# Blocks 2 and 3 of a delta-rule kernel inverted as a pair, their key Grams computed in the head

## The chip, the cores and the metric

The kernel runs on one core of a Trainium2 chip. The metric is the device time of one execution in microseconds (us): 607.63 as the median of three runs of the kernel before (606.84, 611.45, 607.63).

## The reference

The reference computes a delta-rule attention over 4 batches, 8 heads, 768 tokens and head size 48, and puts its output, as 3072 tokens of 384 features, through a feed-forward layer with 2048 hidden features:

```python
k_n = k / (norm(k) + 1e-06)
for t in range(S):
    y[:, :, t] = q[:, :, t] @ state
    v_old = state @ k_n[:, :, t]
    state = state + beta[t] * outer(k_n[:, :, t], v[:, :, t] - v_old)
x = y.transpose(0, 2, 1, 3).reshape(B * S, H * D)
h = x @ w_in
out = maximum(0.01 * h, h) @ w_out
```

Everything is float32.

## The kernel before

**Blocks.** The 768 tokens are cut into 12 blocks of 64. In a block the recurrence of each of the 32 sequences (4 batches by 8 heads) is solved by matrices: the Gram of its 64 keys gives a triangular matrix L, whose inverse T turns keys and values into updates of the state. T is inverted as two halves of 32 tokens each, and the part between them (the corner) is put together afterwards by products with the squares (step pz and pu, L501 and after).

**Per block.** `gram(n)` (L280) loads the keys and queries (kq, L288), multiplies keys with keys and queries in one matmul of 128 columns (pg, L308), copies the key part to gs (ScalarE, L312), stores it to DRAM as gd (L316) and loads it back as L in the layout of the inversion (L346); VectorE masks the query part into rq (L325) and copies the corners into gm (L333). `inv(b)` (L406) eliminates L over 31 steps on VectorE (`eliminate`, L391 and L396). A single block uses 16 columns of T at a time and all 128 partitions; the pair of blocks 0 and 1 uses 32 columns, in one inversion. `solve(n)` (L592) then makes the outputs ys of block n (pk, pw, py, px) and the new state (pc).

**The inverse's way out.** For the pair [0, 1], T is transposed on VectorE (tc, L442, and in place, L448) and copied from there by `place` (L484). For a single block, ScalarE reorders T (L456), SyncE stores it as td and tt (L462, L463), and DMAs load the squares sq (L468, L472) and the halves rt (L537) from these.

**The feed-forward layer.** `ffn(n)` (L739) takes 16 steps of 128 hidden features: ph (L759), Prelu into gh on ScalarE (L769), po (L750). Block 0 takes the weights as plain float32 (one product). From block 1 on inputs, hidden values and weights are each split into a high and a low part, and there are three products, with xl (L128) and gl (L774) as low parts, both made on VectorE.

**Weights.** Eight loads of 1536 KB (wr, `load_w`, L137) bring the weights in a 16-bit layout. Per load j: `pack(j)` (ScalarE, L152), `conv(j)` (four VectorE instructions, L162 to L165), `expand(j)` (ScalarE, L172), `final(j)` (VectorE, L179), after which block 0 can use them; then `cast(j)` (ScalarE, L186) and `lows(j)` (VectorE, L193) make the two parts for block 1 and after. The head issues loads 0 to 3, and 4 to 7 come during block 0.

**What sets the order.** The program is written as generators that are woven by hand: a loop over blocks and over 17 steps s each takes one step of `ffn`, then the work that a table (L860) sets for this step, then steps of `solve` (n + 1), of `inv` and of `gram` by the tables SV, IV, GG and G4. Each engine runs its instructions in the order in which they come out, and `behind(mark)` puts an instruction after a marked one of another engine. All loads and most stores stand in one queue, SyncE's; each of its DMAs waits, by the program's semaphores, for the landing of the one eight places ahead of it. In the head (before block 0): `first()` makes the Grams of blocks 0 and 1, `inv(0)` runs on VectorE beside the loads, `fetch(0, g)` (L570, L572) loads keys, values and queries of block 0, and dummy matmuls (`warm`) run on TensorE towards the end of the inversion.

Of the kernel before, what the change touches and what calls it, by code (L numbers as in the profile page):

```python
# [47 lines left out]
def delta_moe_kernel(ctx: ExitStack, tc, kq0, kqT, kv, qT, beta, cst, w_all, out, nblk):  # L48
# [44 lines left out]
    NB = [[0, 1]] + [[n] for n in range(2, nblk)]  # L93
# [186 lines left out]
    def gram(n):  # L280
        need(sv, "y", n - Q_BUFS // NGR)
        kqs = []
        for g in range(NGR):
            t = sb.tile([P, GS, NPAIR, 2, C], F32, tag="kq", name=f"kq{n}_{g}", bufs=KQ_BUFS)
            kqs.append(t)
            with behind("L" if n > BG + 1 else "kq"):
                for b in range(2):
                    nc.sync.dma_start(t[b * R0:b * R0 + D].rearrange("p s u x t -> p (s u x t)"), kqT[n, g, b])  # L288
        if n == GS:
            yield  # L290
# [4 lines left out]
        for g in range(NGR):  # L295
            kq = kqs[g]
# [3 lines left out]

            ps = [ps_a.tile([P, 512], F32, tag="a", name=f"pg{n}_{g}_{b}") for b in range(2)]
            pv = [x.rearrange("p (u x t) -> p x u t", u=NPAIR, x=2) for x in ps]
            for p in range(NPAIR):
                for c in range(2):
                    for b in range(2):
                        r = slice(b * R0, b * R0 + D)
                        with behind("ph") if n > 2 else nullcontext():
                            nc.tensor.matmul(ps[b][c * 64:(c + 1) * 64, p * 128:(p + 1) * 128],  # L308
                                             kq[r, c ^ b, p, 0], kq[r, c ^ b, p].rearrange("p x t -> p (x t)"),
                                             start=True, stop=True)  # L310
            for b in range(2):
                nc.scalar.copy(gs[:, b], pv[b][:, 0])  # L312
            for c in range(2):
                for e in range(2):
                    a = e * HS + g * GH + c * GU
                    queue.dma_start(  # L316
                        gd[a:a + GU].rearrange("l j i -> j l i"),
                        gs[c * 64 + e * HC:c * 64 + (e + 1) * HC].rearrange("p b u t -> p (b u) t")[:, :, e * HC:(e + 1) * HC])

            def masked(pv=pv, qa=of("q", n, g), to=DATA[g]):  # L320
                for b in range(2):
                    for c in range(2):
                        r = slice(c * 64, (c + 1) * 64)
                        with behind("gl") if n > 2 else nullcontext():
                            nc.vector.tensor_tensor(  # L325
                                qa[to, c, b * NPAIR:(b + 1) * NPAIR], pv[b][r, 1],
                                tri[r].rearrange("p (o t) -> p o t", o=1).broadcast_to([C, NPAIR, C]), ALU.mult)

            def corners(g=g, gs=gs):
                for c in range(2):  # L330
                    k = 2 * g + c
                    with behind("gl") if n > 2 else nullcontext():
                        nc.vector.tensor_copy(gm[n][k * HC:(k + 1) * HC].rearrange("p (b u) t -> p b u t", b=2), gs[c * 64:c * 64 + HC, :, :, HC:])  # L333

            if n == 2:
                masked()
                corners()
            elif not g:
                masked()
                held.append(corners)  # L340
            else:
                tails.extend([[masked], held + [corners]])
                held.clear()
            if g == NGR - 1:
# [4 lines left out]
                if n > GS:  # L349
                    mark["L"] = i.ins  # L350
# [30 lines left out]
    def eliminate(b, L, j, T, m):  # L381
# [13 lines left out]
        for tv, t in parts:  # L395
            mark["steps"] = nc.vector.tensor_tensor(t, t, tv, ALU.subtract).ins  # L396
# [9 lines left out]
    def inv(b):  # L406

        if b:
            need(gg, gram, NB[b][0])
# [4 lines left out]
        if two:  # L414
# [16 lines left out]
        if two:  # L431
            for n in NB[b]:
                lengths(n)
        yield
        for j in range(HC - 1):
            eliminate(b, L, j, T, j + 1 if two else j // 2 + 1)
            if two and j in WARM:
                warm(T[:, 0], WARM[j])
            if j == HC - 2:
                if two:  # L440
# [12 lines left out]
                else:  # L453
                    n = NB[b][0]
                    Tt = X[:, M * HC:].rearrange("p (i m) -> p i m", m=M)
                    nc.scalar.copy(Tt.rearrange("p i m -> p m i"), T)  # L456
                    td = dr.tile([2, HS, HC, HC], F32, tag="td", name=f"td{n}")
                    tt = dr.tile([HS, HC, HC], F32, tag="tt", name=f"tt{n}")
                    Tts[n] = td, tt
                    for x in range(2):  # L460
                        a = x * 64
                        nc.sync.dma_start(tt.rearrange("l i (x m) -> x l i m", m=M)[x], Tt[a:a + HS])  # L462
                        nc.sync.dma_start(td.rearrange("e l m i -> (e l) m i")[:, x::2], T[a:a + 64])  # L463
                    A, B = square(0), square(1)
                    queue = nc.gpsimd if b > BG else nc.sync
                    for k in range(4):
                        r = slice(k * HC, (k + 1) * HC)
                        mark["A"] = queue.dma_start(A[r, :, r], tt[k * GU:(k + 1) * GU].rearrange("u i m -> i u m")).ins  # L468
                    for v in range(4):
                        r = slice(v * HC, (v + 1) * HC)  # L470
                        with behind("A" if b > BG else None):
# [490 lines left out]
```

## Time and profile before

| | before |
|---|---|
| median of 3 runs | 607.63 us (606.84 to 611.45) |
| profiled execution | 607.1 us |
| its span, first to last instruction | 605.3 us |
| TensorE (PE) busy | 564.8 us, 93% |
| VectorE (DVE) busy | 448.7 us, 74% |
| ScalarE (ACT) busy | 311.3 us, 51% |
| GpSimd (POOL) busy | 77.8 us, 13% |
| mean granted TensorE clock | 0.991 |
| share of the chain that ended last | PE 73%, DVE 16%, DMA 4% |

The profile is of one execution. Times in it are us from the first instruction. A timeline row merges neighbouring instructions of one kind: its start, how long the group took, engine, line and operation, output<-input, the shape, and how many; behind it in brackets is how long the engine stood idle before it, and what ended that. The waits view sums such idle times. DMA-issuing instructions stand on their queue's engine (SPq is SyncE's), and the time to landing is given apart. The chain is followed back from the last instruction, step by step, to what released each.

### The profile page before, as it was taken

To read this page: it belongs to the slowest core of one execution; us is meant where nothing else is said; L and a number is where in the kernel's file an instruction comes from. 1 tells how busy PE (TensorE), PEld (TensorE's weight loads), DVE (VectorE), ACT (ScalarE), POOL (GpSimd) and SP (SyncE) were. 2 spreads that over 40 slices of the span, in tenths; PEclk is the share of its full clock that TensorE was granted. 3 is DMA by queue.
4 is the path that set the end of the run, shared out by engine and by line. 5 is a ranking of instruction groups with operands and counts; after the bars stand their busy time and mean duration, and the time that the engine had idled before them with its cause. 6 is when DMAs were issued, how large, how long until landed. Compare 5 with 4: busy or idle time off the path is not lost.

```text
span 605.3 us, 22381 instructions
## 1 busy us (share of the span) xinstructions
PE 564.8 (93%) x9146; PEld 518.2 (86%) x9146; DVE 448.7 (74%) x1981; ACT 311.3 (51%) x786; POOL 77.8 (13%) x135
## 2 busy tenths in 40 slices
PE   5287989889899999999999999999999999999996
PEld 4266767678799999999999999999999999999996
DVE  3999899978848969859859869769779679341221
ACT  3287976744546446436445445445445445454432
POOL 7000000100140040040130130130120210210100
PEclk9987999999999999999999999999999999999999
DMA  5994942244290273381481490490491450410100
GB/s 124 303 286 174 341 95 60 51 86 83 83 187 8 50 118 109 65 182 32 72 181 23 74 194 9 78 195 16 67 195 29 73 123 2 83 34 3 28 1 27
DMA packets 104423, 59.69 MB, mean 99 GB/s; under 512 B 92544, under 2 KB 93632, under 8 KB 103296
## 3 DMA queue, kind: packets, MB, share of 16 engines
q1 hardware_dynamic: 99168, 50.32, 37.5%
q0 software_dynamic: 4576, 7.22, 5.4%
q8 instruction: 72, 1.18, 0.9%
q10 hardware_dynamic: 576, 0.72, 0.6%
q14 instruction: 31, 0.25, 0.2%
HBM read 46.96 MB, written 11.27 MB: 96 GB/s over the span
## 4 chain that ended last, share of the span: by engine, by line
PE 73%; DVE 16%; DMA 4%; issue 3%; ACT 2%; SPq 1%; DVEq 0%; POOL 0%; ACTq 0%
PE po L750 30%; PE ph L759 29%; DVE tmp L391 3%; DVE T L396 3%; PE pw L656 3%; PE py L693 3%; PE pg L308 2%; DVE w L193 2%; DMA tt<-T 2%; PE pk L631 2%; DVE cg L179 2%; PE pc L631 1%; PE px L728 1%; DVE rq L325 1%; DMA sq<-tt 1%
## 5 line engine op out<-in xcount | busy, mean ns | idle before, releaser
L759 PE MATMUL ph<-xh,w 128*128 128x256 f32 x1056 | 203.9, 284 | 0.0
L750 PE MATMUL po<-w,gh 128*128 128x384 f32 x704 | 180.0, 345 | 0.0
L769 ACT ACTIVATE gh<-ph 128x256 fp32r<-128x256 f32 (+1 forms) x192 | 73.5, 385 | 202.6 <-PE ph L759 121.2
L759 PEld LDWEIGHTS ph<-xh,w 128*128 128x128 f32 x1056 | 168.1, 188 | 2.7 <-issue 2.0
L774 DVE TENSOR_TENSOR gl<-ph,gh 128x256 fp32r<-128x256 f32 x176 | 74.3, 423 | 108.4 <-ACT ph L773 103.3
L759 PE MATMUL ph<-xl,w 128*128 128x256 f32 x528 | 148.4, 283 | 1.8 <-DVE xl L128 1.8
L750 PEld LDWEIGHTS po<-w,gh 128*128 128x128 f32 x704 | 120.2, 188 | 3.7 <-issue 1.4
L750 PE MATMUL po<-w,gl 128*128 128x384 f32 x352 | 112.9, 339 | 2.4 <-DVE gl L774 2.4
L396 DVE TENSOR_TENSOR T<-T,tmp 128x60 f32<-128x60 f32 (+35 forms) x661 | 110.8, 207 | 0.7
L391 DVE TENSOR_TENSOR tmp<-T,L 128x60 f32<-128x60 f32 (+35 forms) x661 | 110.8, 208 | 0.6
L759 PEld LDWEIGHTS ph<-xl,w 128*128 128x128 f32 x528 | 99.5, 188 | 2.6 <-DVE xl L128 2.2
L750 PEld LDWEIGHTS po<-w,gl 128*128 128x128 f32 x352 | 65.3, 188 | 3.2 <-DVE gl L774 3.1
L773 ACT ACTIVATE ph<-ph 128x256 f32<-128x256 f32 x176 | 67.0, 380 | 0.0
L468 POOL DMA_DIRECT2D sq<-tt x32 | 18.9, 596 | 281.3 <-PE po L750 97.9
L801 POOL DMA_DIRECT2D out<-ob x44 | 23.3, 533 | 140.1 <-ACT ob L800 138.1
L325 DVE TENSOR_TENSOR rq<-pg,csb 64x256 f32<-64x256 f32 x80 | 33.7, 422 | 3.0 <-ACT gs L312 1.4
L642 ACT ACTIVATE rt<-pk 48x512 f32<-48x512 f32 x44 | 26.0, 592 | 4.4 <-PE pk L631 3.6
L759 PE MATMUL ph<-x,cg 128*128 128x256 f32 x96 | 22.8, 386 | 4.0 <-DVE cg L179 2.4
L759 PEld LDWEIGHTS ph<-x,cg 128*128 128x128 f32 x96 | 17.7, 190 | 8.9 <-DVE cg L179 4.1
L658 ACT COPY rv<-pw 64x384 f32<-64x384 f32 x48 | 22.7, 474 | 3.6 <-PE pw L656 2.4
L647 DVE TENSOR_TENSOR rv<-rv,nt 64x384 f32<-64x384 f32 x44 | 23.2, 551 | 1.4 <-ACT nt L589 0.6
L693 PEld LDWEIGHTS py<-rv,rq 128*32 128x32 f32 x1536 | 19.4, 114 | 5.6 <-ACT rv L658 2.0
(108 smaller groups left out, 620.8 us busy)
## 6 DMA issues: line engine op xcount, KB each, us to landing
wr<-in_w_all SPq DMA_DIRECT2D x8, 1536.0 KB, 13.4
kq<-in_kqT SPq DMA_DIRECT2D x40, 192.0 KB, 6.7
rk<-in_kv SPq DMA_DIRECT2D x24, 192.0 KB, 5.3
rv<-in_kv SPq DMA_DIRECT2D x24, 192.0 KB, 6.0
rq<-in_qT SPq DMA_DIRECT2D x24, 192.0 KB, 3.4
L<-gd SPq DMA_DIRECT2D x18, 256.0 KB, 4.2
out<-ob POOLq DMA_DIRECT2D x44, 96.0 KB, 5.0
td<-T SPq DMA_DIRECT2D x20, 128.0 KB, 3.3
```

What stands on the lines that cost most here:

```text
L325: nc.vector.tensor_tensor(qa[to, c, b * NPAIR:(b + 1) * NPAIR], pv[b][r, 1], tri[r].rearrange("p (o t) -> p o t", o=1).broadcast_to([C, NP ...
L391: nc.vector.tensor_tensor(tv, t[:, :, j:j + 1].broadcast_to([P, k, w]), L[:, j, j + 1:].rearrange("p (o w) -> p o w", o=1).broadcast_to([P ...
L396: mark["steps"] = nc.vector.tensor_tensor(t, t, tv, ALU.subtract).ins
L642: nc.scalar.mul(ts[g][STATE[g], c], pv[g][c * C:c * C + D].rearrange("p (y v) t -> p y v t", y=2), -1.0)
L647: nc.vector.tensor_tensor(v[to, :, us], v[to, :, us], nt[to, g, :, us].rearrange("p h (u o) -> p h u o", o=1).broadcast_to([C, 2, NPAIR, D ...
L693: nc.tensor.matmul(pv[a:a + HC, u * D:(u + 1) * D], qa[:, c, u, e * HC:(e + 1) * HC], v[:, c, u], start=True, stop=True)
L750: i = nc.tensor.matmul(po[t][:, :DO], a[:, ts_], w, start=(f == 0 and k == 0), stop=(f == NFC - 1 and k + 1 == len(ways)))
L759: i = nc.tensor.matmul(ph, w[:, cc * P:(cc + 1) * P], a, start=(k == 0), stop=(k + 1 == len(ways)))
L769: i = nc.scalar.activation(gh, ph, AF.Prelu, alpha=0.01)
L773: i = nc.scalar.activation(ph, ph, AF.Prelu, alpha=0.01)
L774: mark["gl"] = nc.vector.tensor_tensor(gl, ph, gh.bitcast(F32), ALU.subtract).ins
L801: nc.gpsimd.dma_start(out[r0:r0 + C], ob[a:a + C])
```

## The change

Blocks 2 and 3 become a second pair: `inv(1)` inverts both at once with 32 columns, in steps 9 to 17 of block 0 as `inv(1)` of block 2 alone did; block 1 has no inversion then.

- In the head, SyncE loads the keys of blocks 2 and 3 (`ahead_loads`, four loads of 192 KB into the buffer that load 7 of the weights takes later), ahead of all weights; the loads of block 0 stand ahead of the weights too. `ahead(n)` makes the key Grams of both blocks (two times 64 matmuls of 64 columns), ScalarE copies them (eight copies), and SyncE stores them: 16 DMAs into gd and 8 corners into gc.
- `arrive` (step 3 of block 0): GpSimd issues the loads of L and of the corners gm, which VectorE copied before.
- The queries' products of blocks 2 and 3 (64 columns instead of 128) are made in block 1, at its steps 4 and 8, with their masks there.
- The pair's T is transposed twice on VectorE (Tt and Tc), and `fill` copies from these into the squares (two copies on VectorE, the others on ScalarE), and `merge_z` copies the halves on ScalarE: no td, tt, sq and rt DMAs for blocks 2 and 3. The squares are zeroed by GpSimd instead of ScalarE.
- The first three packs stand behind the copies of the Grams. lows(3) moves to the end of block 0, lows(4) to lows(7) spread over block 1 at steps 3, 5, 7 and 9, and the steps of solve(2) in block 1 come later (7 to 14 instead of 4 to 12).

```diff
-    NB = [[0, 1]] + [[n] for n in range(2, nblk)]
+    NB = [[0, 1], [2, 3]] + [[n] for n in range(4, nblk)]
@@ lows
-        with behind("dv"), behind("el2" if j > 2 else None):
+        with behind("gl" if j > 3 else "dv"), behind("sq" if j > 3 else None):
@@ new
+    def ahead_loads():
+
+        t = corner["sb"] = sb.tile([P, 8 * DO], F32, tag="w7", name="k3", bufs=1)
+        keys = t[:, 0:4 * 512].rearrange("p (g i s u x t) -> p g i s u x t", g=NGR, i=2, s=GS, u=NPAIR, x=1)
...
+        for g in range(NGR):
+            for b in range(2):
+                with behind("kq"):
+                    nc.sync.dma_start(keys[b * R0:b * R0 + D, g].rearrange("p i s u x t -> p (i s u x t)"), kq0[2, g, b])
+
+    def ahead(n):
...
+        pv = [products(corner[n][g], [t[:, g * h:(g + 1) * h] for t in ps], corner[n][g], slice(0, 1)) for g in range(NGR)]
...
+        for g in range(NGR):
+            for b in range(2):
+                mark["gs"] = nc.scalar.copy(gs[g][:, b], pv[g][b][:, 0]).ins
+            grams_out(nc.sync, gd, gs[g], g)
+            for c in range(2):
+                nc.sync.dma_start(gc[2 * g + c], gs[g][c * 64:c * 64 + HC].rearrange("p b u t -> p (b u) t")[:, :, HC:])
+        corner[n] = gd, gc
+
+    def arrive():
...
+        for i, n in enumerate(pair):
+            gd, gc = corner[n]
+            nc.gpsimd.dma_start(Lh[b0][i * 64:(i + 1) * 64].rearrange("l j i -> l (j i)"), gd.rearrange("l j i -> l (j i)"))
+        for n in pair:
+            gm[n] = sb.tile([P, GU, HC], F32, tag="gm", name=f"gm{n}", bufs=GM_BUFS)
+            nc.gpsimd.dma_start(gm[n], corner[n][1].rearrange("k p u t -> (k p) u t"))
@@ inv
+                    if two:
+                        Tt, Tc = (sb.tile([P, HC, HS], F32, tag="L", name=f"{x}{b}", bufs=2) for x in ("Tt", "Tc"))
+                        nc.vector.transpose(Tt, T)
...
+                        fill(NB[b][0], 0)
+                        with behind("sq"):
+                            nc.vector.transpose(Tc.rearrange("p l i -> p i l"), T.rearrange("p m i -> p i m"))
+                        square(1)
+                        fill(NB[b][0], 1)
@@ new
+    def fill(n, x):
+
+        Tc, Tt = Tts[n]
+        t = square(x)
+        for k in range(4):
+            r = slice(k * HC, (k + 1) * HC)
+            if n in pair:
+                src = Tc[HC:, k::4] if x else Tt[:, :, k * GU:(k + 1) * GU].rearrange("p m u -> p u m")
+                d = (nc.scalar.copy if x or k % 2 or n != pair[0] else nc.vector.tensor_copy)(t[r, :, r], src)
+                if n == pair[0] and not x and not k % 2:
+                    mark["sq"] = d.ins
+                continue
...
@@ square
-            nc.scalar.mul(t, eye.rearrange("p (o t) -> p o t", o=1).broadcast_to(list(t.shape)), 0.0)
+            nc.gpsimd.memset(t, 0.0)
@@ head
-    for f in range(KA):
-        load_w(f)
     for g in range(NGR):
         fetch(0, g)
-    for f in range(KA, WEARLY):
+    ahead_loads()
+    for f in range(WEARLY):
         load_w(f)
...
+    weave(1, (iv, 2, 0, 1))
+    for n in pair:
+        ahead(n)
     for j in range(NPACK):
-        pack(j)
+        pack(j, "gs")
@@ table of work
-        3: ((expand, 3, "h0_3"),),
+        3: ((expand, 3, "h0_3"), (arrive,)),
...
-        NF + 0: ((lows, 3),), NF + 1: ((lows, 4),),
...
+        NF + 3: ((lows, 4),),
...
-SV = (1, 2, 4, 5, 7, 8, 9), (4, 6, 7, 9, 11, 12), (2, 4, 5, 7, 9, 10, 14), (3, 5, 6, 8, 10, 11, 14)
+SV = (1, 2, 4, 5, 7, 8, 9), (7, 8, 9, 11, 13, 14), (2, 4, 5, 7, 9, 10, 14), (3, 5, 6, 8, 10, 11, 14)
```

The order on three engines shows what moves. First SyncE's queue from the end of the head into block 0. In the kernel before (rq are query loads, cb the constants of block 2, wr weights 4 to 6):

```order
L572 DMA rq_81<-in_qT 48x1024
L363 DMA cb_2060<-in_beta 128x32
L572 DMA rq_78<-in_qT 48x1024
L572 DMA rq_79<-in_qT 48x1024
L137 DMA wr_852<-in_w_all 128x6144
L137 DMA wr_855<-in_w_all 128x6144
L137 DMA wr_1019<-in_w_all 128x6144
```

And in the changed kernel (gd_512 and gd_566 are the Grams of blocks 2 and 3, gc their corners):

```order
L430 DMA cb_2723<-in_beta 128x32
L309 DMA gd_512<-k_256 32x8x32 x4
L354 DMA gc_513<-k_256 256x1x32 x2
L309 DMA gd_512<-k_256 32x8x32 x4
L354 DMA gc_513<-k_256 256x1x32 x2
L309 DMA gd_566<-gs_0_530 32x8x32 x4
L354 DMA gc_567<-gs_0_530 256x1x32 x2
L309 DMA gd_566<-gs_1_531 32x8x32 x4
L354 DMA gc_567<-gs_1_531 256x1x32 x2
L666 DMA rq_78<-in_qT 48x1024
L666 DMA rq_79<-in_qT 48x1024
L137 DMA wr_963<-in_w_all 128x6144
```

The 24 stores now stand between the constants of block 2 and the fourth load of weights.

Second ScalarE in the head, where nt are the key lengths, rv the values that they scale, cg the packed weights and rt<-tc the first copies of the transposed T. In the kernel before:

```order
L152 COPY cg_407<-wr_250 128x1536
L152 COPY cg_409<-wr_252 128x1536
L586 COPY nt_438<-pn_435 128x4x4 x2
L595 ACTIVATE rv_84<-rv_84,nt_438 64x48 x16
L595 ACTIVATE rv_85<-rv_85,nt_438 64x48 x16
L586 COPY nt_476<-pn_473 128x4x4 x2
L152 COPY cg_411<-wr_260 128x1536
L484 COPY rt_82<-tc 32x16x32
```

And in the changed kernel:

```order
L689 ACTIVATE rv_85<-rv_85,nt_437 64x48 x16
L680 COPY nt_475<-pn_472 128x4x4 x2
L351 COPY k_256<-pa_0_478 128x256
L351 COPY k_256<-pa_1_479 128x256
L351 COPY k_256<-pa_0_478 128x256
L351 COPY k_256<-pa_1_479 128x256
L351 COPY gs_0_530<-pa_0_532 128x256
L351 COPY gs_1_531<-pa_0_532 128x256
L351 COPY gs_0_530<-pa_1_533 128x256
L351 COPY gs_1_531<-pa_1_533 128x256
L152 COPY cg_584<-wr_261 128x1536
L152 COPY cg_586<-wr_263 128x1536
```

The copies of the Grams (pa) come in, and all three packs (the third and the copy of T follow next) have moved behind the scaling of the values.

Third VectorE in block 1, where T and tmp are the inversion, w<-cg are the low parts of weights and rq<-pg the masks. In the kernel before, at the beginning of the block:

```order
L128 TENSOR_TENSOR xl_1_1728<-px_0_1715,xh_1_1727 128x256
L396 TENSOR_TENSOR T_1485<-T_1485,tmp_30_1_1717 128x8
L193 TENSOR_TENSOR w_1623<-cg_968,w_1623 128x1536
L391 TENSOR_TENSOR tmp_30_0_1719<-T_1485,L_1077 128x16
L128 TENSOR_TENSOR xl_2_1732<-px_1_1716,xh_2_1731 128x256
L193 TENSOR_TENSOR w_1659<-cg_1027,w_1659 128x1536
L193 TENSOR_TENSOR w_1689<-cg_1213,w_1689 128x1536
L193 TENSOR_TENSOR w_1747<-cg_1280,w_1747 128x1536
L193 TENSOR_TENSOR w_1749<-cg_1445,w_1749 128x1536
```

And in the changed kernel, at the end of the pair's inversion, some six steps into the block:

```order
L463 TENSOR_TENSOR T_1536<-T_1536,tmp_30_0_1831 128x16
L523 STREAM_TRANSPOSE Tt_1837<-T_1536 128x1024
L564 COPY sq_1679<-Tt_1837 32x8x32 x2
L528 STREAM_TRANSPOSE Tc_1838<-T_1536 128x32x32
L193 TENSOR_TENSOR w_1715<-cg_1132,w_1715 128x1536
L322 TENSOR_TENSOR rq_78<-pg_0_1951,csb 64x256 x2
L322 TENSOR_TENSOR rq_78<-pg_1_1952,csb 64x256 x2
L322 TENSOR_TENSOR rq_79<-pg_0_1951,csb 64x256 x2
L322 TENSOR_TENSOR rq_79<-pg_1_1952,csb 64x256 x2
L193 TENSOR_TENSOR w_1745<-cg_1264,w_1745 128x1536
L872 TENSOR_TENSOR gl_6_2025<-ph_73,gh_6_2023 128x256
```

The differences of weights no longer stand in a row ahead of the first gl; the two transposes and the copies into the square have come in between the elimination and lows(4).

## Rows read from the trace of the kernel before

**Rows 1.** The page's 40 slices of 15.1 us: tenths of TensorE busy.

```profile
PE   5287989889899999999999999999999999999996
```

**Rows 2.** Timeline, TensorE: the first products of FFN 1 and of FFN 2.

```profile
114.79 0.69 PE L759 MATMUL ph<-xh,w 128*128 128x256 f32 x2
...
171.18 0.28 PE L759 MATMUL ph<-xh,w 128*128 128x256 f32 x1
```

**Rows 3.** Waits, TensorE, 105 to 175 us: total, times, longest (us).

```profile
PE po L750 <- DVE gl L774: 2.4, 2, 1.4
PE pc L668 <- issue: 1.9, 1, 1.9
PE ph L759 <- DVE xl L128: 1.8, 2, 1.2
PE pz L501 <- DMA sq<-tt: 0.5, 1, 0.5
```

**Rows 4.** Timeline, VectorE, block 1: four lows in a row.

```profile
118.95 6.75 DVE L193 TENSOR_TENSOR w<-cg,w 128x1536 fp32r<-128x1536 f32 x4
```

**Rows 5.** Chain, 116 to 142 us: start, us, what (the two DMA steps).

```profile
131.68 4.41 DMA tt<-T
...
137.50 2.33 DMA sq<-tt
```

**Rows 6.** Timeline, ScalarE, head: scaling of values, pack(2), first copy of T.

```profile
29.91 7.40 ACT L595 ACTIVATE rv<-rv,nt 64x48 f32<-64x48 f32 x32
...
37.34 1.62 ACT L152 COPY cg<-wr 128x1536 bf16<-128x1536 bf16 x1
39.60 0.62 ACT L484 COPY rt<-tc 32x512 f32<-32x512 f32 x1 [0.64 <-DVE tc L442]
```

**Rows 7.** Timeline, ScalarE, block 0: pack(4), and two Gram copies.

```profile
62.40 1.61 ACT L152 COPY cg<-wr 128x1536 bf16<-128x1536 bf16 x1
...
73.51 0.65 ACT L312 COPY gs<-pg 128x256 f32<-128x256 f32 x2
```

**Rows 8.** The page's 40 slices: GB/s moved by DMA.

```profile
GB/s 124 303 286 174 341 95 60 51 86 83 83 187 8 50 118 109 65 182 32 72 181 23 74 194 9 78 195 16 67 195 29 73 123 2 83 34 3 28 1 27
```

**Rows 9.** Timeline, SyncE's queue: constants, query loads, w4 to w6, stores of one block.

```profile
44.18 0.35 SPq L363 DMA_DIRECT2D cb<-in_beta  x1
49.80 2.28 SPq L572 DMA_DIRECT2D rq<-in_qT  x2
54.02 5.54 SPq L137 DMA_DIRECT2D wr<-in_w_all  x3
...
122.91 3.78 SPq L316 DMA_DIRECT2D gd<-gs  x8
```

**Rows 10.** Lines 137 and 316 alone: issue to landing of weights, then of stores.

```profile
DMA to landing us min/median/max: 6.1/13.4/16.9
DMA to landing us min/median/max: 1.6/2.4/7.5
```

**Rows 11.** Timeline, VectorE, block 0: masks and corners of the first half.

```profile
74.22 1.75 DVE L325 TENSOR_TENSOR rq<-pg,csb 64x256 f32<-64x256 f32 x4
76.00 0.58 DVE L333 COPY gm<-gs 32x256 f32<-32x256 f32 x2
```

**Rows 12.** Timeline, TensorE: the product behind final(5); key and query products.

```profile
89.55 2.86 PE L759 MATMUL ph<-x,cg 128*128 128x256 f32 x12 [2.44 <-DVE cg L179]
...
120.60 1.98 PE L308 MATMUL pg<-kq 48*64 48x128 f32 x64
```

**Rows 13.** Timeline, VectorE, head: a step of the pair's elimination, the two transposes.

```profile
25.88 0.49 DVE L391 TENSOR_TENSOR tmp<-T,L 128x136 f32<-128x136 f32 x2
...
37.36 2.15 DVE L442 STREAM_TRANSPOSE tc<-T 128x1024 f32<-128x1024 f32 x1
39.54 1.25 DVE L448 STREAM_TRANSPOSE T<-T 128x1024 f32<-128x1024 f32 x1
```

More of the change, by code (lines that the diff above doesn't have):

```diff
@@ new lines, in grams_out, with masked @@
+    def grams_out(queue, gd, gs, g):
+        for c in range(2):
+            for e in range(2):
+                a = e * HS + g * GH + c * GU
+                queue.dma_start(
+                    gd[a:a + GU].rearrange("l j i -> j l i"),
+                    gs[c * 64 + e * HC:c * 64 + (e + 1) * HC].rearrange("p b u t -> p (b u) t")[:, :, e * HC:(e + 1) * HC])
+    def masked(n, g, pq, *gates):
+        qa, to = of("q", n, g), DATA[g]
+        for b in range(2):
+            for c in range(2):
+                r = slice(c * 64, (c + 1) * 64)
+                with ExitStack() as gate:
+                    for x in gates:
+                        gate.enter_context(behind(x))
+                    nc.vector.tensor_tensor(
+                        qa[to, c, b * NPAIR:(b + 1) * NPAIR], pq[b][r],
+                        tri[r].rearrange("p (o t) -> p o t", o=1).broadcast_to([C, NPAIR, C]), ALU.mult)
@@ new lines, in gram @@
+    def gram(n):
+        if n in pair:
+            if n != pair[0]:
+                load_kq(n, "kq")
+            need(sv, "y", n - Q_BUFS // NGR)
+            ps = [ps_a.tile([P, 512], F32, tag="a", name=f"pg{n}_{b}") for b in range(2)]
+            h = NPAIR * C
+            pv = [products(kqs[n][g], [t[:, g * h:(g + 1) * h] for t in ps], kqs[n][g], slice(1, 2), "ph") for g in range(NGR)]
+            for g in range(NGR):
+                masked(n, g, [t[:, 0] for t in pv[g]], "gl", "sq")
+                yield
+            return
+        need(sv, "y", n - Q_BUFS // NGR)
+        load_kq(n, "L" if n > NS else "kq")
@@ L299, in gram, with masks @@
                 gm[n] = sb.tile([P, GU, HC], F32, tag="gm", name=f"gm{n}", bufs=GM_BUFS)
[L301 to L310, printed above, removed]
+            pv = products(kqs[n][g], [ps_a.tile([P, 512], F32, tag="a", name=f"pg{n}_{g}_{b}") for b in range(2)], kqs[n][g], slice(0, 2), "ph")
             for b in range(2):
                 nc.scalar.copy(gs[:, b], pv[b][:, 0])
[L313 to L327, printed above, removed]
+            grams_out(queue, gd, gs, g)
+            def masks(g=g, pq=[t[:, 1] for t in pv]):
+                masked(n, g, pq, "gl")
             def corners(g=g, gs=gs):
@@ L331, in corners @@
                     k = 2 * g + c
-                    with behind("gl") if n > 2 else nullcontext():
+                    with behind("gl"):
                         nc.vector.tensor_copy(gm[n][k * HC:(k + 1) * HC].rearrange("p (b u) t -> p b u t", b=2), gs[c * 64:c * 64 + HC, :, :, HC:])
[L335 to L339, printed above, removed]
+            if not g:
+                masks()
                 held.append(corners)
             else:
-                tails.extend([[masked], held + [corners]])
+                tails.extend([[masks], held + [corners]])
                 held.clear()
@@ L394, in eliminate @@
             parts.append((tv, t[:, :, j + 1:]))
-        for tv, t in parts:
-            mark["steps"] = nc.vector.tensor_tensor(t, t, tv, ALU.subtract).ins
+        for x, (tv, t) in enumerate(parts):
+            mark["steps"] = mark[f"step{x}"] = nc.vector.tensor_tensor(t, t, tv, ALU.subtract).ins
     def warm(x, count):
@@ L687, in step_y @@
         def step_y(g):
+            if n == pair[0]:
+                with behind("rv"):
+                    fill(pair[1], g)
             qa, v = of("q", n, g), of("v", n, g)
```

129 lines of the change are left out of this document (80 added, 49 removed).

## The prediction

> **What bounds the kernel now.** I read the page's slices first, then the PE's waits, then the timelines of ScalarE, SyncE and VectorE in the head and in blocks 0 and 1. The reader is to see in the PE slices [rows 1] that from slice 12 on (166 us) TensorE stands at 9 in every slice but the last: there it is nearly the bound, and little that the change does off TensorE can be worth anything. What can be won or lost lies before: in the head, block 0 and block 1. FFN 1 begins at 114.79 and FFN 2 at 171.18 [rows 2], so block 1 takes 56.4 us. In this block TensorE waits 6.6 us in four ways [rows 3]: 2.4 for gl, 1.9 for nothing that is shown, 1.8 for xl, 0.5 for the DMA that fills the square of block 2. The first and the third have one cause: four differences of low parts stand in a row on VectorE, 6.75 us [rows 4], and xl and gl queue behind them. The DMA hop (tt 4.41, sq 2.33 [rows 5]) is long, but only 0.5 us of it is waited for [rows 3].
>
> So the question is what block 1 gives back and what the head and block 0 pay. A shift of FFN 2's beginning passes unchanged to the end. The profiled execution took 607.1 us with a span of 605.3; the median of the three runs is 607.63, so I add 0.5 to a sum made on the profile.
>
> **The head.** Four key loads of 192 KB now go out ahead of all weights, and the six loads of block 0 too. On ScalarE the three packs stand behind eight copies of Grams, which stand behind the 32 multiplications. Before, pack(2) ran at 37.34, straight after the multiplications (29.91 to 37.31), and the copy of the transposed T at 39.60 waited only for VectorE [rows 6]. Now 7.40 of multiplications, eight copies at 0.33 (0.65 for two [rows 7]) and three packs at 1.62 make 14.9 us in a row ahead of this copy. It starts on time only if the multiplications begin by 24.7. If they begin at 29.91, as before, it starts at 44.8: +5.2, the upper end. If the loads of block 0, which no longer follow two weights of 1536 KB, let them begin by 24.7, the bound is w2: 0.79 MB more stand ahead of it, at 286 to 303 GB/s [rows 8] 2.6 to 2.8 us. It landed by 37.34, so by 40.1 at the latest now, and pack(2) ends at 41.7: +2.1. Where w2 had landed early enough, nothing: 0, the lower end. A gain is excluded, since VectorE's inversion, which sets 39.60, is the same. I take +2.5, near the middle of the three. The 128 Gram products of the two blocks run while TensorE is mostly idle (slice 2 of [rows 1], at 2).
>
> **Block 0: w4 behind the stores.** This is the term that I weigh most. The 24 stores of Grams and corners stand on SyncE after the constants of block 2 and ahead of the q loads and of w4 to w6. Before, the constants went out at 44.18, two q loads at 49.80 and w4 at 54.02 [rows 9]. Each DMA waits for the landing of the one eight places ahead, which is why the q loads went at 49.80. I let the first store go at 48. Eight stores of the same form took 3.78 us [rows 9], so 24 take 11.3: 59.3. Two q loads at up to 2.28 together bring w4 to 61.5 instead of 54.02. The ends: 54.02 itself, if SyncE gets to the stores early enough, and 72.8, if the stores go at the pace of their landings (below). w4 lands no sooner than 6.1 us after its issue [rows 10]: 67.6. Pack(4), which ran at 62.40 without a wait for a DMA [rows 7], then runs at 67.6, 5.2 late; behind it on ScalarE stand the copies of block 1's T, gh of step 3, and the expansion of the third weight, and through these final(3) on VectorE, for which TensorE waits.
>
> Part of this comes back before final(5). The masks (1.75 for four) and corner copies (0.58 for two) of both Gram halves leave block 0 [rows 11], 4.7 us of VectorE, and two pairs of Gram copies, 1.3 of ScalarE. If VectorE sets the pace, the 5.2 shrinks to 0.5; if ScalarE does, to 3.9. I take +2.5 at final(5), between the two. The head's +2.5 is not added: conversions 0 to 3 run into the wait for w4. TensorE waited 2.44 us for final(5) before ph at 89.55 [rows 12], so it has no reserve there, and FFN 1 begins at 114.79 + 2.5 = 117.3.
>
> One rule of the Trainium skill speaks against the stores (DMA: Bandwidth & Descriptors, section Specifications): under 512 bytes a transfer falls short of the line rate, because the engine reads, changes and writes back. The stores go in rows of 32 floats, 128 bytes. The rows here show that stores of this form land in 1.6 to 7.5 us, median 2.4 [rows 10], which at eight in flight keeps pace with their issue; by the rule the longer end would hold, and the time would be the third rival's.
>
> **Block 1.** Take X for the beginning of FFN 1. The pair's elimination costs what the pair [0,1] cost in the head: from the step at 25.88 to the transpose at 37.36 11.5 us are left at X [rows 13]. Three xl and six gl at 0.42 stand between, 3.8 us. Then one transpose at 1.25, two copies into the square at about 0.25, the other transpose at 2.15 [rows 13], lows(4) at 1.7 (6.75 for four [rows 4]), the masks 1.75, lows(5) 1.7 and gl of step 6 0.4: X + 24.8. TensorE without waits reaches the product with this gl after some seven steps of 16; (56.4 - 6.6)/16 is 3.1 each, so X + 22. It loses 2 to 3 us there, at lows(4) or at this gl; the chain is one, so these waits do not add. I take 2. The bounds are 0 (the elimination further on at X, since it has all of block 0's last steps) and 7 (ScalarE's copies of squares and halves delay gh too).
>
> The products of q with k for blocks 2 and 3 have half the columns of those that took 1.98 [rows 12]; half of it and all of it bound them, I take 1.3 for each, nearer the half: 2.6 in place of 1.98, +0.6. The old waits of 6.6 go: no four lows in a row, no DMA hop, and solve 2 five steps later, away from the wait of 1.9. Block 1 then takes 56.4 - 6.6 + 0.6 + 2.0 = 52.4, from 117.3 to 169.7, against 171.18: -1.5. The zeroing of the squares goes to GpSimd, which has nothing else to do there; it frees ScalarE, at no gain that ends on TensorE. From block 2 on nothing changes but the place of Grams.
>
> Sum: 607.1 - 1.5 = 605.6, on the scale of the median 606.1, say 606.
>
> **The rivals.** First: w4 isn't late, because SyncE reaches the stores early or w4's pack has slack. Then only the head's 0 to 2.5 is paid, and 4.7 us of VectorE are gone from a stretch that VectorE limits. Final(5) comes 2.2 earlier with the head's delay, TensorE's 2.44 shrinks, FFN 1 begins at 112.6, FFN 2 at 165.0: -6.2, 601. Without the head's delay it is 2.4 better: 599. For it speaks that ScalarE had nothing to wait for before pack(4) at 62.40 though w4 went at 54.02, some 2 us in hand at a landing of 6.1; against it, that 11.3 us of stores stand in a queue kept in order.
>
> Second, the slower side: the stores land slowly, and from a landing of 3.8 us (eight at 0.47) on, the landings set the pace of SyncE, not the issues. At 7.5 us each, the longest seen [rows 10], three rounds take 22.5: w4 at 72.8, landed at 78.9, pack(4) 16.5 late. Less the 4.7 of VectorE and some 2 of idle time, FFN 1 begins 10 late, at 124.8, FFN 2 at 177.2: +6.0, 613.6 on the median. Against it speaks the median of 2.4; for it, that w3 and the loads of block 2 are under way on the same rings.
>
> Third: the chain at the end of the pair's inversion replaces the wait it removes. With 7 in place of 2 in block 1 the sum is 611. For it speaks that TensorE's next low weight, the square and gl 6 now hang on one engine in one order; against it, that a wait at the square is filled by the FFN's products in the queue.
>
> Fourth, the DMA hop was hidden: that is so by [rows 3] for all but 0.5 and is in the sum.
>
> **How the numbers follow.** About 1% (6 us) is what a measurement of this kernel can tell from no change. Forecast 0.44 (602 to 609), first rival 0.26, second 0.17, third 0.13. Faster by over 1% (under 601.5) takes most of the first and the low edge of the forecast: 0.28. Slower (over 613.7) takes half of the second, a third of the third and a little of the forecast's edge: 0.18. The rest is 0.54. The range goes from 597, under which only the best of the first rival lies, to 614.
>
> **What would show it.** In the profile after: the issue of w4 at 61 to 62 and pack(4) with a wait for a DMA; the copy of T in the head near 42; FFN 1 at 117, FFN 2 near 170; in block 1 no wait for xl, and 2 us for lows or gl. FFN 1 before 113.5 would say that the stores cost nothing; a w4 after 66, that landings set their pace; waits of 5 us in block 1, that the pair's chain is the new bound. If a slice of TensorE from the twelfth on falls under 9, the whole argument is wrong.

## The result, and the profile after

The changed kernel takes 616.40 us (median of 4, 615.23 to 617.72), the kernel before on the same chip 608.77: a ratio of 1.0123, 95% interval 1.0074 to 1.0172. It is 1.2% slower, where no change was forecast. The profiled execution took 617.04 us with a span of 615.3, 10.0 more than before.

The places of the prediction, in both traces (us from the start; "FFN n" is its first product):

| | before | predicted | after |
|---|---|---|---|
| first copy of T in the head | 39.60 | 42.1 | 42.16 |
| FFN 0 | 53.31 | | 57.36 |
| w4 issued | 54.02 | 61.5 | 65.47 |
| pack(4) | 62.40 | 67.6 | 72.43 |
| FFN 1 | 114.79 | 117.3 | 119.72 |
| FFN 2 | 171.18 | 169.7 | 180.72 |
| last instruction ends | 605.3 | | 615.3 |

So block 0 and the head cost 4.9 us and block 1, which was to give some back, 4.6 more: 61.0 in place of 56.4. The 0.5 that is left of the 10 comes in later blocks. The page's slices of TensorE answer to [rows 1], and below them is its granted clock in tenths:

```profile
PE   5578898996999999999999999999999999999996
...
PEclk9995999997989999999999999999999999999999
```

The clock before:

```profile
PEclk9987999999999999999999999999999999999999
```

From slice 12 on TensorE stands at 9 as before; the loss lies ahead of it, in slices 3, 5, 7 and 10, which are lower than before. The clock was low in the head before too (41.3 to 51.6 us), but now it is low for longer there (44.1 to 61.2), and twice more in slices 10 and 12. These are single executions: the one of the kernel before that was traced has a mean clock of 0.991, its other executions have 0.975 to 0.991, and the four of the changed kernel 0.974 to 0.980. By windows of 10 us (columns: busy time of TensorE, its weight loads, VectorE, ScalarE, GpSimd, then granted clock, DMA share, GB/s):

```profile
50.00:60.00 10.00, 8.80 (x205) 7.20 (x200) 8.53 (x16) 6.70 (x12) 0.69 (x1) 0.50 0.34 53
...
140.00:150.00 10.00, 5.00 (x66) 3.95 (x70) 9.11 (x14) 6.34 (x17) 0.95 (x1) 0.83 0.01 2
150.00:160.00 10.00, 10.00 (x260) 9.11 (x257) 8.18 (x16) 4.77 (x12) 0.00 (x0) 0.83 0.37 80
...
170.00:180.00 10.00, 10.00 (x122) 9.45 (x115) 5.34 (x15) 4.79 (x13) 4.71 (x8) 0.83 0.60 146
```

0.50 is the lower of the two levels, 1.2 of 2.4 GHz. At 140 to 150 TensorE is busy for only 5.0 of 10 us: that is the stretch in which block 1 waits. In it the clock fell, at 146.5, and it rose again at 153.3; from 170.4 to 173.8 it was low once more.

**SyncE's queue**, which answers to [rows 9] (start, us, queue, line, operation):

```profile
47.05 2.85 SPq L309 DMA_DIRECT2D gd<-k  x4
49.98 1.32 SPq L354 DMA_DIRECT2D gc<-k  x2
...
61.80 1.21 SPq L354 DMA_DIRECT2D gc<-gs  x2
63.11 2.27 SPq L666 DMA_DIRECT2D rq<-in_qT  x2
65.47 1.32 SPq L137 DMA_DIRECT2D wr<-in_w_all  x3
```

The first store went at 47.05 (I said 48), but the 24 took 16.0 us, 0.67 each, not 0.47. The eight corners (gc) went 0.62 apart: 1.2 us more than eight at 0.47. Among the stores SyncE also waited 2.3 us, which its waits show (44 to 67 us; total, times, longest):

```profile
SPq L309 <- ACT rv L753: 1.2, 1, 1.2
SPq L309 <- DMA rv<-in_kv: 0.7, 1, 0.7
...
SPq L309 <- ACT ys L793: 0.4, 1, 0.4
```

Why a store waits for these copies of ScalarE is not shown. On ScalarE, the head and pack(4), answering to [rows 6, 7]:

```profile
39.53 1.61 ACT L152 COPY cg<-wr 128x1536 bf16<-128x1536 bf16 x1 [1.53 <-DMA wr<-in_w_all]
42.16 1.26 ACT L553 COPY rt<-tc 32x512 f32<-32x512 f32 x2 [1.02 <-DVE tc L509]
...
72.43 1.55 ACT L152 COPY cg<-wr 128x1536 bf16<-128x1536 bf16 x1 [4.56 <-DMA wr<-in_w_all]
74.00 2.52 ACT L553 COPY rt<-tc 32x512 f32<-32x512 f32 x4
```

Pack(4) now waits 4.56 us for w4, and the copies of block 1's T stand behind it. But the first copy of T, at 42.16, had ended its wait for pack(2) at 41.14: it waited 1.02 more for VectorE. There the elimination looks like this (line 458 multiplies, 463 subtracts):

```profile
31.85 0.26 DVE L463 TENSOR_TENSOR T<-T,tmp 128x99 f32<-128x99 f32 x1
32.15 0.26 DVE L458 TENSOR_TENSOR tmp<-T,L 128x96 f32<-128x96 f32 x1
32.44 0.26 DVE L463 TENSOR_TENSOR T<-T,tmp 128x96 f32<-128x96 f32 x1
...
34.99 0.38 DVE L463 TENSOR_TENSOR T<-T,tmp 128x110 f32<-128x110 f32 x2
...
38.15 0.22 DVE L458 TENSOR_TENSOR tmp<-T,L 128x56 f32<-128x56 f32 x1
...
40.02 2.06 DVE L509 STREAM_TRANSPOSE tc<-T 128x1024 f32<-128x1024 f32 x1
```

Before, two instructions for the two halves of T stood side by side to the end (x2 in every row up to this one), and the transpose began at 37.36 [rows 13]:

```profile
36.58 0.31 DVE L396 TENSOR_TENSOR T<-T,tmp 128x15 f32<-128x15 f32 x2
```

Now from 31.85 on one half is worked alone, 0.3 us from one instruction to the next, each on the result of the last; from 36.5 on the other half follows alone. Why: the dummy products of the head read the first column of T, which belongs to that other half, and stand on TensorE behind the new Gram products of block 3:

```profile
32.04 2.25 PE L300 MATMUL pa<-k 48*64 48x64 f32 x43 [2.06 <-issue]
34.22 0.63 PE L468 MATMUL warm<-T,csb 128*128 128x32 f32 x2
```

That half may not be written before the read is done, at 34.8, and the row of 34.99 is the first that writes it. The transpose is 2.66 us late by this, not by pack(2).

**Block 1.** The waits of TensorE, 119 to 181 us, which answer to [rows 3] (total, times, longest):

```profile
PE po L848 <- DVE gl L872: 3.6, 1, 3.6
PE ph L857 <- DVE w L193: 1.7, 1, 1.7
PE pg L300 <- issue: 1.3, 1, 1.3
PE ph L857 <- DVE xl L128: 1.1, 2, 0.7
```

7.7 us, where the old ones were 6.6. The first two hang on VectorE's chain at the end of the pair's inversion:

```profile
135.41 1.25 DVE L523 STREAM_TRANSPOSE Tt<-T 128x1024 f32<-128x1024 f32 x1
136.76 0.79 DVE L564 COPY sq<-Tt 32x256 f32<-32x256 f32 x2
137.58 2.17 DVE L528 STREAM_TRANSPOSE Tc<-T 128x1024 f32<-128x1024 f32 x1
139.65 1.72 DVE L193 TENSOR_TENSOR w<-cg,w 128x1536 fp32r<-128x1536 f32 x1
141.40 3.47 DVE L322 TENSOR_TENSOR rq<-pg,csb 64x256 f32<-64x256 f32 x8
144.88 1.76 DVE L193 TENSOR_TENSOR w<-cg,w 128x1536 fp32r<-128x1536 f32 x1
146.67 0.42 DVE L872 TENSOR_TENSOR gl<-ph,gh 128x256 fp32r<-128x256 f32 x1
```

The elimination ends 15.7 us after FFN 1 begins (I had 15.3), but gl of step 6 is ready at 27.4, not 24.8: the masks are eight, 3.47 us and not 1.75, and the copies into the square took 0.79, not 0.5. TensorE had nothing left from 143.6 to 147.15.

### The profile page after: what moved, and what is told of

Read it like the earlier page. It is cut to its first block, busy times and chain, and to the rows that moved or that the text cites. A ratio compares the mean times of both kernels' runs of the same rounds, so it can differ in the third digit from the quotient of the medians.

```text
span 615.3 us, 22490 instructions
## 1 busy us (share of the span) xinstructions
PE 574.2 (93%) x9274; PEld 526.4 (86%) x9274; DVE 438.4 (71%) x1841; ACT 319.2 (52%) x802; POOL 82.3 (13%) x141
## 4 chain that ended last, share of the span: by engine, by line
PE 77%; DVE 12%; ACT 4%; issue 3%; DMA 3%; POOL 1%; DVEq 0%; SPq 0%; ACTq 0%; POOLq 0%
PE ph L857 31%; PE po L848 30%; PE pw L751 3%; PE py L791 3%; DVE tmp L458 3%; PE pg L300 3%; DVE T L463 3%; PE pk L726 2%; ACT cg L152 1%; PE px L826 1%; PE pc L726 1%; DMA wr<-in_w_all 1%; DVE w L193 1%; PE pu L588 1%; DMA sq<-td 1%
## 5 line engine op out<-in xcount | busy, mean ns | idle before, releaser
L463 DVE TENSOR_TENSOR T<-T,tmp 128x16 f32<-128x16 f32 (+14 forms) x602 | 103.7, 210 | 1.0
L458 DVE TENSOR_TENSOR tmp<-T,L 128x16 f32<-128x16 f32 (+14 forms) x602 | 103.5, 210 | 0.9
L857 PE MATMUL ph<-x,cg 128*128 128x256 f32 x96 | 24.5, 408 | 2.2 <-DVE cg L179 1.9
L857 PEld LDWEIGHTS ph<-x,cg 128*128 128x128 f32 x96 | 19.0, 204 | 6.6 <-DVE cg L179 2.8
L128 DVE TENSOR_TENSOR xl<-px,xh 128x256 fp32r<-128x256 f32 x33 | 13.0, 421 | 14.6 <-ACT xh L127 14.6
```

Source lines behind the costliest of these rows:

```text
L458: nc.vector.tensor_tensor(tv, t[:, :, j:j + 1].broadcast_to([P, k, w]), L[:, j, j + 1:].rearrange("p (o w) -> p o w", o=1).broadcast_to([P ...
L463: mark["steps"] = mark[f"step{x}"] = nc.vector.tensor_tensor(t, t, tv, ALU.subtract).ins
L857: i = nc.tensor.matmul(ph, w[:, cc * P:(cc + 1) * P], a, start=(k == 0), stop=(k + 1 == len(ways)))
```

## The experiments

Twelve kernels, each against runs of the kernel before on its chip. The groups of four ran on three different chips, so versions of different groups are compared by their ratios. Each trace is of one execution, up to 3.5 us from the median of its kernel. The first three take one suspected cost away each, the fourth all three.

**Dummy products off T.**

```diff
-                warm(T[:, 0], WARM[j])
+                warm(eye[:, 0:HC], WARM[j])
```

> The dummy matmuls in the head read a constant instead of the first column of T. Theory 1 (the inversion in the head is late because this read stands on TensorE behind the new Gram products, so that half of T may not be written and VectorE works the other half alone): the elimination runs in pairs again, the transpose of T starts at 37.4 us instead of 40.0, the first copy of T at 41.2 (then behind the third pack) instead of 42.2, the first product of FFN 0 at 55 to 56 instead of 57.4. If w4 behind the stores then sets block 0, FFN 1 still begins at 119 to 120 and the time stays within 1 us of 616.4; if the head sets it, 614 to 615. Rival (the new copies on ScalarE or VectorE's own speed make the inversion late): transpose still at 40.0, no change.

Measured: 615.24 us, ratio 1.0105 (1.0068 to 1.0142), not apart from the changed kernel. The elimination runs in pairs again and the transpose begins at 37.09, so the read of T is what split it. But FFN 0 begins at 57.42, as late as with it. The 1.6 us gained at the copy of T (40.61) are lost again some 5 us further on; the chain there shows (start, us, what):

```profile
45.17 1.43 PE pw L751 x61
46.60 3.06 issue
49.66 1.42 PE pw L751 x59
```

This gap, for which the trace shows no wait, was 1.54 in the changed kernel and ended at the same time, 49.81. So in these two traces the head does not end by the copy of T.

**Stores on GpSimd.**

```diff
-            grams_out(nc.sync, gd, gs[g], g)
+            grams_out(nc.gpsimd, gd, gs[g], g)
-                nc.sync.dma_start(gc[2 * g + c], gs...)
+                nc.gpsimd.dma_start(gc[2 * g + c], gs...)
```

> The 24 stores of Grams and corners are issued by GpSimd instead of SyncE. Theory 1 (w4 stands behind the stores): w4 goes out at about 57, when its gate on VectorE opens, instead of 65.5, the fifth pack runs at 63.5 to 65 instead of 72.4, FFN 1 begins at 115 to 117 instead of 119.7, the time is 612 to 614. Rival 1 (ScalarE and VectorE pace block 0, w4 only adds idle time in front of it): pack earlier, but FFN 1 at 118.5 or later, 615 to 616. Rival 2 (the stores slow the other loads wherever they are issued): w4 lands late still, no change.

Measured: 609.83 us, ratio 1.0013 (0.9990 to 1.0036): 6.6 us back, the largest of the three and below theory 1's 612 to 614. w4 goes out at 57.60, near theory 1's 57, and pack(4) waits for no DMA:

```profile
57.60 5.54 SPq L137 DMA_DIRECT2D wr<-in_w_all  x3
```

```profile
68.58 1.60 ACT L152 COPY cg<-wr 128x1536 bf16<-128x1536 bf16 x1
```

FFN 1 begins at 115.92 (as theory 1 has it, though pack(4) came later than it said), and block 1 takes 61.9, no less than in the changed kernel. The stores themselves are still slow: GpSimd issues the first at 30.0 and the last at 71.8. Up to FFN 2 no wait of TensorE in this trace is put down to them.

**Masks late.**

```diff
-GG = ... ((4, 5), (8, 9))
+GG = ... ((7, 8), (9, 10))
```

> The products of q with k for block 2 and their masks come three steps later in block 1 (step 7 instead of 4, the second at 9 instead of 8). Theory 1 (one chain on VectorE, transposes, lows, masks, lows, gl of step 6, makes TensorE wait 5.3 us, and this wait lets its clock fall to half for 6.8 us): the wait for gl goes, that for the low weights falls to 0 to 1.7, no stretch at half clock at 147 us, block 1 takes 54 to 57 us instead of 60.8, the time is 610 to 613. Rival (the wait moves to the next low weight or to the masks' readers): block 1 at 59.5 or more, 615 to 617.

Measured: 611.96 us, ratio 1.0056 (1.0035 to 1.0077): 4.4 us back. Block 1 takes 56.4 (122.58 to 178.93), the wait for gl is gone, and in block 1 the clock stays at its upper level up to 168.8 (it is low for 3.4 us there). FFN 1 itself began 2.9 later here than in the changed kernel, though nothing ahead of it was edited; so the traces show the gain in the length of block 1, not in the place of FFN 2. The first three waits of its block 1:

```profile
PE ph L857 <- DVE w L193: 1.4, 1, 1.4
PE pg L300 <- issue: 1.4, 1, 1.4
PE ph L857 <- DVE xl L128: 1.1, 2, 0.7
```

**All three.**

> All three edits together. If the three terms are independent and as theory 1 has them: FFN 1 at 113 to 116, block 1 54 to 57, 605 to 609. If one of them hides another: 609 to 613.

Measured: 605.95 us, ratio 0.9961 (0.9932 to 0.9990): 10.5 us under the changed kernel and a little under the kernel before. The time is inside what independent terms give; FFN 1 at 116.1 and a block 1 of 57.3 are just above it.

The next four asked what was left. Three stand on the kernel with the three edits. In the first, the fourth weight load leaves the head's stretch:

```diff
-WEARLY, NPACK, NG = 4, 3, 5
+WEARLY, NPACK, NG = 3, 3, 5
     conv(0)
+    load_w(3, "dv")
```

> On top of the kernel with the three edits, the fourth weight load goes out only after the first conversions (about 49 us), so that the DMA engines are free from about 43 us on. Theory (in the head TensorE's own instructions come late because their load stands behind weights, the unexplained gap of 1.5 to 3.1 us between products of pw): the gap falls to 1.2 or less, the first product of FFN 0 comes at 54 to 55.5 instead of 56.5, the time is 603.5 to 605 against 605.95. Rival (the gap is TensorE's own and has nothing to do with other transfers): gap as before, first product at 56.5, no change, or slower by the later fourth pack.

Measured: 609.37 us, ratio 0.9996 (0.9964 to 1.0029): no gain, a miss on time (the ratio is above the 0.9961 of the three edits, but the intervals overlap). Pack(2) waited for w2 until 42.27, and FFN 0 began at 58.84. The gap in pw did go, but pw itself ran on from 48.85 only, 2.6 later than with the three edits, and another gap came a product later, while w3 was under way:

```profile
PE py L791 <- issue: 2.7, 1, 2.7
```

Then the steps of solve 2 back at their old places:

```diff
-SV = ..., (7, 8, 9, 11, 13, 14), ...
+SV = ..., (4, 6, 7, 9, 11, 12), ...
```

> On top of the kernel with the three edits, the steps of solve 2 in block 1 go back to their old places (4, 6, 7, 9, 11, 12). Theory (with the late places pw, py, pc and the Grams of block 4 come together, a stretch of small products in which TensorE's clock falls to half for 3.4 to 6.8 us): no half clock after 155 us, block 1 takes 54 to 55.5 instead of 57.1, the time is 603 to 605. Rival (the late places are there since the inverse comes late; then TensorE waits for it): waits at pk or pw of 2 us or more in block 1, 606 to 608.

Measured: 609.03 us, ratio 1.0003 (0.9978 to 1.0028). The old places gain nothing (the intervals overlap here too): block 1 took 58.3 in this trace (113.68 to 172.02), 57.3 with the three edits, with the wait for low weights up from 1.4 to 2.3, and the clock fell twice there even so. The rival's waits at pk or pw were not there either: 1.2 in all for pw. The theory of small products is not borne out by it.

> Both edits on top of the three. If both theories hold and add: 601.5 to 604. If the first gains nothing at the end: as the run with the old places of solve 2, within 1 us.

Measured: 614.45 us, ratio 1.0073 (1.0037 to 1.0109). Together the two edits lose 1.1% to the three edits alone, more than the intervals; both theories failed on time.

And one on the changed kernel itself, dummy products in block 1's wait:

```diff
                     first_product(f + e, bank[:, e])
+                if n == 1 and f == 8:
+                    warm(eye[:, 0:HC], 10)
```

> The changed kernel with one small and ten large dummy products (about 3.3 us at full clock) in block 1 just where TensorE waits for low weights and gl of step 6. Theory (the wait costs twice: 5.3 us itself, and some 3 us by the half clock that follows it for 6.8 us): with TensorE busy through the wait the clock stays at full level from 140 to 154, gl of step 6 is reached as late as before (147 to 148), block 1 takes 57 to 58.5 instead of 60.8, the time is 613 to 614.5 against 616.4. Rival (the clock falls because of the small products pu, pg and pk that follow): half clock as before, time 616 to 618.

Measured: 617.50 us, ratio 1.0133 (1.0084 to 1.0181), no better. The dummy products ran at 141.1 to 143.6, in the first wait; a second one of 2.7 us remained behind them, and the clock stood at the lower level from 147.6 to 154.4, much as in the changed kernel:

```profile
PE po L848 <- DVE gl L874: 2.7, 1, 2.7
```

So this run does not settle whether the wait or the small products that follow it bring the clock down. In the run with the masks late the same products (pu, pg, pk) follow no wait for gl, and the clock stays up from 130 to 160; that speaks for the wait, but pg stands elsewhere there. Nor does a long wait always stand ahead of a fall: with the three edits the clock fell at 160.3, for 6.8 us, behind waits of 0.8 and 0.5 us for pg; in the run with the third pack behind the copies of T (below) the same block 1 ran with waits of 1.1 and 0.3 there, and its clock did not fall. What decides it stays open.

The last four test the head.

**Stores and masks, dummy products on T as in the changed kernel.**

> The stores on GpSimd and the masks late, but the dummy products reading T as in the changed kernel. Theory (once w4 is on time, the head sets block 0, so that the split inversion counts): 607 to 609, 1.5 to 2.5 slower than the 605.95 with all three. Rival (the head's late inversion is hidden behind TensorE's gap in pw whatever the rest): within 1 us of 606.

Measured: 604.93 us, ratio 0.9924 (0.9892 to 0.9956). The rival was right on the time: with the inversion as late as in the changed kernel (transpose at 40.02) it is no worse than with it mended. The ratio is the lowest of the versions tried, 0.8% under the kernel before, but its interval overlaps that of the three edits. The rival's reason does not show in this trace: the gap in pw is only 0.4, and FFN 0 begins at 55.58, 13.4 after the copy of T. Its FFN 1 begins at 112.41 and its FFN 2 at 167.24, so block 1 takes 54.8:

```profile
112.41 0.69 PE L857 MATMUL ph<-xh,w 128*128 128x256 f32 x2
...
167.24 0.40 PE L857 MATMUL ph<-xh,w 128*128 128x256 f32 x2
```

**Third pack behind the first copies of T**, on the three edits:

```diff
-    for j in range(NPACK):
+    for j in range(NPACK - 1):
         pack(j, "gs")
     weave(1, (iv, NI - 2, 0, 1))
+    pack(NPACK - 1, "place")
```

> On top of the three edits the third pack stands behind the first copies of T instead of ahead of them: the copy of T at 39.3 to 39.8 instead of 41.2. Theory (TensorE's instructions arrive at about 48 whatever comes before, so an earlier copy of T only lengthens the gap in pw): gap 3.5 to 4 instead of 2.2, the first product of FFN 0 at 56 to 56.6 as before, time within 1 us of 606. Rival (the copy of T sets the head): first product at 54.5 to 55, 604 to 605.

Measured: 605.67 us, ratio 0.9944 (0.9919 to 0.9969), no change, as the theory has it. The copy of T comes at 39.55, as early as before the change, FFN 0 at 56.52, and the gap takes the difference:

```profile
PE pw L751 <- issue: 3.8, 1, 3.8
```

**Keys and queries of block 2 loaded in the middle of block 0**, on the three edits:

```diff
-        load_kq(pair[0], "kq")
+    def late_keys():
+        load_kq(pair[0], "h0_8")
...
+        9: (..., (late_keys,)),
```

> On top of the three edits, the keys and queries of block 2 (four loads of 192 KB, which the head asks for behind the weights) are loaded in the middle of block 0. Theory (less data in the queues at 44 to 48, so TensorE's instructions come earlier): the gap in pw at 1.2 to 1.6 instead of 2.2, first product at 55 to 56, time 604 to 605.5. Rival (these loads are not in the way, or w4 now meets them): no change, 605.5 to 607.

Measured: 607.10 us, ratio 0.9961 (0.9936 to 0.9985), no change. But the edit did not do what it was meant to. The four loads went out not in the middle of block 0 but at the very start of the kernel (with the three edits they go from 31.4 to 46.2):

```profile
1.67 3.74 SPq L290 DMA_DIRECT2D kq<-in_kqT  x4
```

So they did leave the stretch of 44 to 48, but the inversion began later (its first copy into T at 18.20, with the three edits 15.99), and the transpose came at 39.77. The gap in pw is gone altogether, and FFN 0 begins at 55.55 with a copy of T as late as 42.89: 12.7 us from the one to the other, where the changed kernel took 15.2 and the kernel before 13.7. These are all the waits of TensorE in its head from 40 us on but two shorter than 0.5:

```profile
PE pz L608 <- ACT rt L556: 3.2, 1, 3.2
PE py L794 <- issue: 0.5, 1, 0.5
```

The gap's end cannot be read from its absence: pw ran on from 47.87 here, 1.7 later than with the three edits, which alone takes most of their 2.2.

> Both edits on top of the three. If the copy of T and the instructions both bound the head: first product at 53.5 to 54.5 as in the kernel before, FFN 1 at 112 to 114, time 602 to 604. If only one does: as the better of the two single runs.

Measured: 607.02 us, ratio 0.9961 (0.9936 to 0.9986). Not what either theory said: the four loads went out at 1.65 here too, the inversion began later still (19.29), the transpose of T at 40.87, and the copy of T came no earlier than 43.04. Neither theory was put to the test by this run.

## Why the prediction was wrong

Three steps failed where it counts: the 24 stores, priced at 11.3 us, took 16.0; the waits at the end of the pair's inversion were 5.3 us, not 2; and TensorE's clock stood at nothing in the sum and cost block 1 about 3.

**The head: the number right, the reason wrong.** I had the copy of T at 42.1 for pack(2); it came at 42.16 for VectorE, so the agreement is luck (by pack(2) alone it would have come at 41.14). The step that failed is "A gain is excluded, since VectorE's inversion, which sets 39.60, is the same". The inversion has the same instructions, but not in the same order, and the order of the changed kernel could be read before it ran. A wait on TensorE, through a read of T in dummy products, had come into VectorE's chain. And no cost of it can be measured: with or without it the ratios are 1.0123 and 1.0105 with the stores on SyncE, 0.9924 and 0.9961 with the stores and masks moved. In the first two, the traces show why: a gap in TensorE's stream behind it ends at the same time (49.81 and 49.66) and fills up what is gained.

**w4: the mechanism right, the size too small.** The failing term is "24 take 11.3": they took 16.0, w4 went out 11.5 us late, not 7.5, and pack(4) 10 late, not 5.2. It priced all 24 as stores of Grams that wait for nothing; the eight corners cost more each, and SyncE waited 2.3 us among them. Of the excess of 4.7 that leaves 1.2 open. The second rival's rule (landings set the pace from 3.8 us on) was not the reason: the head's stores of Grams landed in 2.0 us by the median, corners in 2.9, and no landing took over 4.2. "I take +2.5 at final(5)" followed: VectorE finished the weights of load 5 at 96.9, against 89.5 before, +7.4. What I let come back before final(5), 2.7, was right (2.6); that another 2.5 came back behind it, so that FFN 1 was 4.9 late, I did not have. Taking the stores off SyncE gave 6.6 us. Two readings in this part are wrong without bearing on the sum. The q loads of the kernel before went at 49.80 because they waited up to 4.9 us for TensorE's py, not for a landing eight places ahead. And the sentence on transfers under 512 bytes names the third rival, but slow landings and their 613.6 are the second.

**Block 1: an error of count, and a cost left out.** The chain was laid out right, but with "the masks 1.75": that is one half of a block, and both halves stand there, 3.47. TensorE lost 5.3 at lows(4) and gl, not "2 to 3 us ... I take 2"; xl kept 1.1 of its 1.8 and another 1.3 without a shown wait stayed, where "The old waits of 6.6 go". The sum put the clock at nothing: the lower level from 146.5 to 153.3 and 170.4 to 173.8 is in none of its terms. Of the products of q with k one group took 1.16 us at the upper level, near my 1.3, and the other 1.99 at the lower.

Against the predicted 169.7 for FFN 2 that makes 11.0: 2.4 from FFN 1 (119.72 for 117.3) and 8.6 from block 1 (61.0 for 52.4), of which 5.7 are waits (7.7 for 2.0). The rest, 2.9, is work that took longer. The windows of block 1 show what of it is the clock (the changed kernel, the three edits, and the third pack behind the copies of T):

```profile
119.72:180.72 61.00, 53.32 (x861) 48.51 (x860) 44.60 (x133) 32.90 (x82) 7.79 (x13) 0.92 0.28 66
116.11:173.40 57.29, 53.27 (x860) 49.08 (x859) 43.56 (x129) 32.66 (x82) 8.88 (x15) 0.94 0.30 76
116.10:170.27 54.17, 50.23 (x860) 46.21 (x859) 43.53 (x129) 32.64 (x82) 7.42 (x13) 1.00 0.32 78
```

The last has no stretch at the lower level, and the same products keep TensorE busy for 50.2 us, which is my sum without its waits (56.4 - 6.6 + 0.6 = 50.4); in the changed kernel they take 3.1 more. The second and third rows have the same block 1 and 3.8 and 4.0 us of waits, and differ by 3.1 us with 6.8 us at the lower level.

**The rivals.** The third, the chain at the end of the inversion, came true with its waits; the second in its direction, by w4, though not by landings; I had set them against each other, and they came together. Their prices add within the noise: 6.6 and 4.4 in the single runs, 11.5 in the run with both, which was on another chip (1.1%, 0.7% and 2.0% by the ratios).

**What the change is worth.** Without its two costs the pair is a small gain: the kernel with the three edits and the last four lie 0.4 to 0.8% under the kernel before, each with its interval. The idea held; two places in queues did not.

## What to carry to other kernels

A block of new instructions is paid by what stands behind it in its queue: before pricing 24 small stores, list what the same queue issues next and who waits for that, and put them on a queue whose next customer is far. When an order is made by a scheduler, read the order of the engine that sets the path too, although its instructions are the same: a read of the tile on another engine can split its pairs. And count the instructions of a chain that ends in a wait one by one, by the shapes in the order, not by a row that showed half of them. When an edit moves a load, look up in the trace where it went before reading anything from the time.

## What was not expected of the hardware

TensorE's gap in the head. In all fourteen traces, each gap without a shown wait in pw and py ended 1.3 to 1.6 us after a 16 KB packet of kind "instruction" was through, 24 gaps in all. In the changed kernel and in the run with the dummy products off T (start of the packet, how long it took, end of the gap):

```
changed kernel     47.20  1.34   49.81
dummies off T      47.02  1.29   49.66
```

In the first, TensorE was out of work at 48.27, in the second at 46.60, and the end is the same. From 44 to 48 us the DMA engines were at 1.04 of their time in the changed kernel and at 0.34 in the kernel before, whose gap was 1.2. That the data in flight make the packet late would fit this, but it is not shown: no run delayed the packet alone. With the keys of block 2 loaded at the start, 0.79 MB less at that time, the packet began at 46.72, only 0.4 earlier than with the three edits (47.12); in the run with the stores and masks moved, which loads the keys as the changed kernel does, it began at 46.44. What the traces do show is that while such a packet sets the end of the gap, a shorter chain ahead of it gains nothing.
